# The 64-row remainder of wo, shared between tiles three and four of each query block

## The chip, the core and the metric

One core of a Trainium2 chip runs the whole kernel in one launch. The metric is device time in microseconds (us): the median of several executions. The profiler records one further execution, and its times are given from the start of that execution's span.

## What is computed

A transformer layer whose two branches run side by side on the same normalised input. There are 2048 tokens, a width of 448, 16 heads of 28, an attention window of 256, and a feed-forward width of 1792.

```python
def _A_ref(x, wqkv, wo):
    ...
    scores = jnp.einsum("bhqd,bhkd->bhqk", q, k) * (Dh ** -0.5)
    mask = (idx[:, None] - idx[None, :] >= 0) & (idx[:, None] - idx[None, :] < W)
    scores = jnp.where(mask[None, None], scores, -1e9)
    p = _softmax(scores, axis=-1)
    o = jnp.einsum("bhqk,bhkd->bhqd", p, v)
    return (lambda x, *d: x.transpose(*d))(o, 0, 2, 1, 3).reshape(B, S, D) @ wo
def _B_ref(x, w_gate, w_up, w_down):
    return (_gelu(x @ w_gate) * (x @ w_up)) @ w_down
x = A_x
xn = _layernorm(x, axis=-1)
return x + _A_ref(xn, A_wqkv, A_wo) + _B_ref(xn, B_w_gate, B_w_up, B_w_down)
```

## The kernel before

The tokens are worked on in four query blocks of 512, `qb` 0 to 3, each of four tiles (`tt` 0 to 3) of 128 tokens. Every engine executes its instructions in the order in which the program issues them; no scheduler reorders them (`manual_schedule`).

For each block there is an attention stage of ten steps (four heads at a time, `steps_of`), then a gated stage (`gated`). In a step TensorE computes the scores `sc` into the only score buffer (L653), ScalarE takes the exponential (L657) into `p_sb`, and VectorE multiplies the edges by masks (`apply_masks`, L573). While ScalarE works, TensorE executes what the list `plan` holds for that step: `(g, n)` is n further pieces of a generator. One generator, `gen_pairs`, projects q, k and v of the next block; another, `gen_up`, is the up half of the feed-forward of the last block (tile `ue`); and `gen_down(qb - 1)` is the output of the block before. So the output of blocks 0, 1 and 2 is computed in the attention of blocks 1, 2 and 3, and the output of block 3 alone at the end of the kernel.

`gen_down` makes the output of a 128-token tile as one sum in PSUM, `po`, 448 wide: 14 terms of `wd` with the gated hidden layer `hT`, and 4 terms of `wo` with the attention's output `oN`. 448 rows are three and a half times 128, so the fourth `wo` term has only 64 rows. `o_finish` (L357) prepares it on GpSimd. For blocks 0 to 2 it copies those 64 rows of tile 1 into the upper 64 partitions, and clears these for tiles 2 and 3. Tiles 0 and 1 then do their 64-row terms as a pair (L408): one in the upper, one in the lower half of the array's rows. Tiles 2 and 3 each do a 128-row term of which half is zero. In block 3 the upper half is cleared for all tiles and all four terms have 128 rows. Tile 3 of block 3 is computed in two halves of 224 columns, `first` and `last`, in tiles called `pl`, so that only a narrow add and store are left at the end. `end` adds the input `x_sb` to the sum on VectorE (L381, tile `res`) and issues the store on SyncE (L384).

PSUM has four banks for `po`, `pq`, `pk`, `pv`, `ov`, `ue` and `u`. `take` takes the bank that was given back first, `give` puts one back at the end of the list; both happen as the program is written out, and on the chip a matmul that starts a sum in a bank waits until the bank's last reader is done.

Of the kernel before, what the change touches and what calls it, by code (L numbers as in the profile page):

```python
# [17 lines left out]
P = 128  # L18
# [9 lines left out]
def kernel(  # L28
# [328 lines left out]
    def o_finish(qb):  # L357

        oN = oNs[qb]
        if qb < NB - 1:  # L360
            nc.gpsimd.memset(oN[64:128, 3, 2 * P:QB], 0.0)
            nc.gpsimd.tensor_copy(out=oN[64:128, 3, P:2 * P], in_=oN[0:64, 3, P:2 * P])
        else:
            nc.gpsimd.memset(oN[64:128, 3, :], 0.0)

    def gen_down(qb):

        hT, oN = hTs[qb], oNs[qb]
        fs = [(hT, wd, f) for f in range(NF)]
        main, late, os = fs[0:5] + fs[7:12], [fs[f] for f in (5, 12, 6, 13)], [(oN, wo, g) for g in range(4)]  # L370

        def begin(tt, lo=0, up=D):
            return tt, take("po", up - lo), lo, up

        def end(tt, po, lo, up):
            t, w = 4 * qb + tt, up - lo
            if lo:
                res = work.tile([P, 2 * QB], bf16, name="res", tag="wa", bufs=1)
            else:
                res = work.tile([P, D], bf16, name="res", bufs=4)  # L380
            nc.vector.tensor_tensor(out=res[:, 0:w], in0=po[:, 0:w], in1=x_sb[:, t, lo:up], op=ALU.add)  # L381
            if id(po) in held:
                give(po)
            nc.sync.dma_start(out=outv[:, t, lo:up], in_=res[:, 0:w])  # L384
            last_res[:] = [res]

        def part(o, terms, start=False, stop=False):
            tt, po, lo, up = o
            w = up - lo
            for n, (x, wt, k) in enumerate(terms):  # L390
                nc.tensor.matmul(po[:, 0:w], lhsT=x[:, k, tt * P:(tt + 1) * P], rhs=wt[:, k, lo:up],  # L391
                                 start=start and n == 0, stop=stop and n == len(terms) - 1, skip_group_check=True)
                if stop and n == len(terms) - 1:
                    end(*o)
                yield

        def whole(terms, *o):
            yield from part(begin(*o), terms, True, True)

        if qb < NB - 1:  # L400
            two = [begin(tt) for tt in range(2)]
            for o in two:
                yield from part(o, main + late, True)
            for o in two:
                yield from part(o, os[0:3])
            for tt, po, *_ in two:
                r = slice(64 * tt, 64 * tt + 64)
                nc.tensor.matmul(po, lhsT=oN[r, 3, tt * P:(tt + 1) * P], rhs=wo[r, 3, :], start=False, stop=True,  # L408
                                 tile_position=(64 * tt, 0), skip_group_check=True)
            for o in two:  # L410
                end(*o)
            yield
            for tt in (2, 3):
                yield from whole(main + late + os, tt)
        else:
            two = [begin(tt) for tt in range(2)]
            for terms, start in ((main, True), (late, False)):
                for o in two:
                    yield from part(o, terms, start)
            first, last = ((3, phase[0].pool.tile([P, 2, QB], f32, name="pl", tag="s")[:, 0, 0:D // 2], lo, lo + D // 2)  # L420
                           for lo in (0, D // 2))
            yield from part(first, main + late, True)
            for o in (*two, first):
                yield from part(o, os, False, True)
            yield from part(last, main, True)
            yield from whole(main + late + os, 2)
            yield from part(last, late + os, False, True)

    def new_hT(qb):
# [156 lines left out]
    def attention(qb, plan):  # L586
# [54 lines left out]
        for i, (scores, ncol, edges) in enumerate(steps):  # L641
            assert (qb, scores[-1][0]) in done
            if i in pvs:
                pv(pvs[i])
            while fresh:
                apply_masks(*fresh.pop(0))
            ss = phase[0].pool.tile([P, 4, QB], f32, name="sc", tag="s")
            p_sb = work.tile([P, 4, QB], bf16, name="p_sb", bufs=5)
            for g, half, kt, q0, nq, col in scores:
                k0, nk = (64 * half, 64) if half is not None else (0, P)  # L650
                for j in range(4):
                    r = slice(32 * j, 32 * j + Dh)
                    nc.tensor.matmul(ss[k0:k0 + nk, j, col:col + nq], lhsT=kT[r, g, kt * P + k0:kt * P + k0 + nk],  # L653
                                     rhs=qT[r, g, ring(qb).start + q0:ring(qb).start + q0 + nq], start=True, stop=True,
                                     tile_position=(32 * j, k0), skip_group_check=True)
                parts.setdefault(g, []).append((half, kt, q0, nq, col, p_sb))
            nc.scalar.activation(out=p_sb[:, :, 0:ncol], in_=ss[:, :, 0:ncol], func=ACT.Exp, scale=SCALE)  # L657
            flush()
            if qb:
                fresh.append((p_sb, edges))  # L660
            else:
                for m in edges:
                    masked(p_sb, *m)
            while later:
                scale_o(*later.pop(0))
            for n in plan[i]:
                if n == "sums":
                    sums()
                elif n == "inverse":
                    inverse()  # L670
                elif n == "masks":
                    apply_masks(*fresh.pop(0))
                elif n == "scale":
                    scale_o(*later.pop(0))
                if not isinstance(n, tuple):
                    if callable(n):
                        n()
                    continue
                for _ in range(n[1]):
                    next(n[0], None)  # L680
# [120 lines left out]
    for qb in range(NB):  # L801
# [4 lines left out]
        if qb == 0:  # L806
            new_hT(0)
            early = (0, 1, 2, 3, 4)
            u = chain(gen_qk((1, 2, 3), {1: (3, pvs[3]), 2: (2, pvs[2])}), gen_up(0, (1, 2, 3, 0, 4), (3, 4)))
            w = gen_pairs(1, (("v", 0), ("v", 2), ("k", 0), ("k", 1), ("k", 2)))  # L810
            plan = [[(u, 2), ahead, (u, 1)], [lambda: v_dense(2, pvs[2]), (u, 2), ahead2, (u, 1)],
                    [lambda: spare.append(spare.pop(1)), (u, 2), ahead3, (u, 4)], [lambda: stat(8), (u, 11)],
                    [lambda: stat(9), (u, 7), lambda: stat(10), (u, 7), lambda: fill_pads(True)], ["sums", (u, 7)],
                    ["inverse", "scale", (w, 11)], [(w, 10)],
                    [lambda: stat(11), (w, 7), lambda: rstd(8, 4), "sums", "inverse", (w, 7)]]
        else:
            d = gen_down(qb - 1)
            if qb < 3:
                u = gen_pairs(qb + 1, (("v", 0), ("k", 0), ("v", 2), ("k", 1), ("k", 2)))
                plan = [[(d, 14)], [(d, 11)], [(d, 11)], [(u, 7)], [(d, 18)], ["sums", (u, 7), "inverse"], [(u, 11)],  # L820
                        [lambda: q_last(qb + 1, nc.vector.tensor_copy), (d, 6), "sums"], [(d, 2), "inverse", (d, 10)],
                        [(u, 9), "masks", (u, 1)]]
                plan[3] = [(d, 1), (u, 7)]
                if qb == 2:
                    plan[0], plan[2] = [(d, 13)], [(d, 10)]
                if qb == 1:
                    for i, j in enumerate((0, 1, 2, 4)):
                        plan[j].insert(0, lambda t=12 + i: stat(t))
                    plan[4].append(lambda: rstd(12, 4))
                    plan[1] = plan[1][:1] + [lambda: q_last(1, nc.vector.tensor_copy), (d, 8)]  # L830
                    plan[2] = plan[2][:1] + [(d, 12), lambda: collect(1)]
                    plan[4].append(lambda: deliver(1))
            else:
                new_hT(3)
                early = (1, 2, 3, 4, 5, 6)
                u = gen_up(3, early, (4, 6))
                plan = [[(u, 12)], [(u, 9)], [(d, 12)], [(d, 10)], [(d, 12)], [(d, 1), (u, 7), "sums"], [(d, 12), "inverse"],
                        ["sums", "inverse", (d, 12)], [(d, 12)], [(u, 13), "masks", (u, 1)]]
        if qb in (1, 2):
            swap(qb + 1)  # L840
        score_pool(1)
# [186 lines left out]
```

## Time and profile before

| | us |
|---|---|
| median of 3 runs | 213.64 (213.34 to 214.03) |
| the profiled execution's own time | 213.22 |
| its span, first to last instruction | 211.5 |
| TensorE busy in it | 206.6 |
| VectorE busy | 156.8 |
| ScalarE busy | 131.6 |
| GpSimd busy | 48.9 |

A row of the timeline gives the start, the time from the first instruction's start to the last one's end, the engine, the line, the operation and how many instructions are merged; in brackets stands how long the engine sat idle before it and what released it. On TensorE consecutive matmuls overlap in these records, so what one costs is the distance between starts, not its duration. A row of the chain of waits gives start, length, engine, tile, line and count.

### The profile page before, as it was taken

To read this page: it belongs to the slowest core of one execution; us is meant where nothing else is said; L and a number is where in the kernel's file an instruction comes from. 1 tells how busy PE (TensorE), PEld (TensorE's weight loads), DVE (VectorE), ACT (ScalarE), POOL (GpSimd) and SP (SyncE) were. 2 spreads that over 40 slices of the span, in tenths; PEclk is the share of its full clock that TensorE was granted. 3 is DMA by queue.
4 is the path that set the end of the run, shared out by engine and by line. 5 is a ranking of instruction groups with operands and counts; after the bars stand their busy time and mean duration, and the time that the engine had idled before them with its cause. 6 is when DMAs were issued, how large, how long until landed. Compare 5 with 4: busy or idle time off the path is not lost.

```text
span 211.5 us, 6340 instructions
## 1 busy us (share of the span) xinstructions
PE 206.6 (98%) x2682; PEld 97.4 (46%) x2682; DVE 156.8 (74%) x355; ACT 131.6 (62%) x123; POOL 48.9 (23%) x86
## 2 busy tenths in 40 slices
PE   7999999999999999999999999999999999999994
PEld 2333444444454545444445444544444454544562
DVE  6899988999767985696437897395384699659722
ACT  4699488566677977413778787523577786757000
POOL 5388658451100220041000112013000022005100
PEclk9999999999999999999999999999999999999999
DMA  6999989969410101003521000100100011000011
GB/s 167 289 236 203 108 212 221 220 189 223 111 47 29 39 11 34 9 4 67 74 75 47 25 0 27 22 0 16 31 3 0 10 41 41 7 3 0 22 60 39
DMA packets 24889, 15.67 MB, mean 74 GB/s; under 512 B 9208, under 2 KB 24728, under 8 KB 24856
## 3 DMA queue, kind: packets, MB, share of 16 engines
q1 hardware_dynamic: 23814, 14.87, 32.3%
q8 instruction: 22, 0.36, 0.7%
q10 hardware_dynamic: 1042, 0.34, 0.7%
q14 instruction: 11, 0.09, 0.2%
HBM read 9.26 MB, written 2.41 MB: 55 GB/s over the span
## 4 chain that ended last, share of the span: by engine, by line
PE 94%; DVE 2%; ACT 1%; DMA 1%; issue 0%; DVEq 0%; ACTq 0%
PE po L391 24%; PE gt L457 20%; PE u L457 12%; PE ue L457 8%; PE pq L333 7%; PE sc L653 7%; PE ov L625 5%; PE pv L319 4%; PE pq L190 2%; PE pl L391 2%; DVE st L155 1%; DMA x_sb<-in_A_x_dram 1%; PE pv L190 1%; ACT p_sb L657 1%; PE s L190 1%; PE pk L190 1%
## 5 line engine op out<-in xcount | busy, mean ns | idle before, releaser
L657 ACT ACTIVATE p_sb<-sc 128x2048 bf16<-128x2048 f32 x39 | 73.2, 1878 | 20.6 <-PE sc L653 14.4
L497 ACT ACTIVATE p_sb<-gt 128x1024 bf16<-128x1024 f32 x28 | 28.7, 1024 | 33.7 <-PE gt L457 30.7
L592 POOL TENSOR_TENSOR oN<-oc,l 128x512 bf16<-128x512 f32 x16 | 21.6, 1354 | 119.0 <-DVE l L605 119.0
L457 PE MATMUL gt<-xnT,wg 64*128 64x512 bf16 x224 | 45.6, 376 | 0.0
L391 PE MATMUL po<-wd,hT 128*128 128x448 bf16 x210 | 43.3, 353 | 0.0
L457 PE MATMUL gt<-xsw,wg 64*128 64x512 bf16 x168 | 40.7, 376 | 0.0
L505 DVE TENSOR_TENSOR hT<-p_sb,u 128x512 bf16<-128x512 bf16 x34 | 21.9, 677 | 16.0 <-PE u L457 15.8
L573 DVE TENSOR_TENSOR p_sb<-p_sb,masks 128x256 bf16<-128x256 bf16 (+1 forms) x90 | 27.8, 364 | 7.6 <-ACT p_sb L657 7.6
L391 PEld LDWEIGHTS <-hT 128*128 128x128 bf16 x238 | 21.9, 98 | 19.4 <-issue 2.2
L457 PEld LDWEIGHTS <-wg 64*128 64x128 bf16 x392 | 19.0, 94 | 22.5 <-issue 0.2
L457 PEld LDWEIGHTS <-wu 64*128 64x128 bf16 x392 | 18.8, 94 | 22.4 <-issue 1.0
L457 PE MATMUL u<-xnT,wu 64*128 64x512 bf16 x136 | 28.1, 376 | 0.0
L457 PE MATMUL u<-xsw,wu 64*128 64x512 bf16 x102 | 24.7, 376 | 0.0
L457 PE MATMUL ue<-xnT,wu 64*128 64x512 bf16 x88 | 18.0, 377 | 0.0
L381 DVE TENSOR_TENSOR res<-po,x_sb 128x448 bf16<-128x448 f32 x15 | 9.0, 619 | 11.5 <-PE po L391 11.0
L653 PE MATMUL sc<-qT,kT 28*64 28x320 bf16 (+7 forms) x648 | 16.4, 261 | 0.1
L457 PE MATMUL ue<-xsw,wu 64*128 64x512 bf16 x66 | 16.3, 377 | 0.0
L583 POOL TENSOR_SCALAR_AFFINE_SELECT p_sb<-p_sb 128x512 bf16<-128x512 bf16 (+1 forms) x21 | 14.2, 705 | 5.9 <-ACT p_sb L657 5.8
L610 DVE TENSOR_TENSOR oc<-oc,ov 128x512 f32<-128x512 f32 x12 | 8.2, 681 | 8.6 <-ACT oc L609 8.6
L653 PEld LDWEIGHTS <-kT 28*64 28x64 bf16 (+1 forms) x648 | 7.5, 102 | 13.3 <-issue 12.0
L474 DVE CAST hT<-ue 128x512 bf16<-128x512 f32 x18 | 11.6, 679 | 1.8 <-PE ue L457 1.8
L391 PE MATMUL po<-wo,oN 128*128 128x448 bf16 x54 | 12.0, 352 | 0.0
(110 smaller groups left out, 278.9 us busy)
## 6 DMA issues: line engine op xcount, KB each, us to landing
out_dram<-res SPq DMA_DIRECT2D x15, 112.0 KB
wd<-in_B_w_down_dram SPq DMA_DIRECT2D x2, 784.0 KB
x_sb<-in_A_x_dram SPq DMA_DIRECT2D x3, 448.0 KB
xsw<-xnT SPq DMA_DIRECT2D x6, 192.0 KB
wu<-in_B_w_up_dram SPq DMA_DIRECT2D x4, 224.0 KB
wg<-in_B_w_gate_dram SPq DMA_DIRECT2D x2, 448.0 KB
wu<-in_B_w_up_dram SPq DMA_DIRECT2D x2, 336.0 KB
wg<-in_B_w_gate_dram SPq DMA_DIRECT2D x2, 336.0 KB
```

What stands on the lines that cost most here:

```text
L190: nc.tensor.matmul(ps, lhsT=lhs(c), rhs=rhs(c), start=start and c == 0, stop=stop and c == 2, skip_group_check=True)
L333: nc.tensor.matmul(ps, lhsT=w.rearrange("p h d -> p (h d)"), rhs=xchunk(qb, hi, c, qb * QB, QB), start=c == 0, stop=c == 6, tile_position= ...
L391: nc.tensor.matmul(po[:, 0:w], lhsT=x[:, k, tt * P:(tt + 1) * P], rhs=wt[:, k, lo:up], start=start and n == 0, stop=stop and n == len(term ...
L457: nc.tensor.matmul(ps, lhsT=w[64 * hi:64 * hi + 64, c, p * P:(p + 1) * P], rhs=xchunk(qb, hi, c, qb * QB, QB), start=c == 0, stop=c == 6, ...
L474: copy(out=hTs[qb][:, p + 7 * i, :], in_=us[i])
L497: nc.scalar.activation(out=ges[p][:, :, :], in_=gt[:, :, :], func=ACT.Gelu_apprx_tanh)
L505: nc.vector.tensor_tensor(out=hT[:, p + 7 * i, :], in0=ge[:, i, :], in1=u, op=ALU.mult)
L573: nc.vector.tensor_tensor(out=reg, in0=reg, in1=m, op=ALU.mult)
L583: nc.gpsimd.affine_select(out=reg, in_=reg, pattern=mid + [[1 if diag else -1, min(w, P)]], compare_op=ALU.is_ge, fill=0.0, base=0 if diag ...
L592: nc.gpsimd.tensor_tensor(out=oN[:, g, :], in0=oc[:, :], in1=inv, op=ALU.mult)
L653: nc.tensor.matmul(ss[k0:k0 + nk, j, col:col + nq], lhsT=kT[r, g, kt * P + k0:kt * P + k0 + nk], rhs=qT[r, g, ring(qb).start + q0:ring(qb) ...
L657: nc.scalar.activation(out=p_sb[:, :, 0:ncol], in_=ss[:, :, 0:ncol], func=ACT.Exp, scale=SCALE)
```

## The change

- `o_finish`: one GpSimd copy of the 64 rows of tiles 1 and 3 into the upper half, for every block; both clearings go.
- `gen_down` for blocks 0 to 2: three 128-row `wo` terms for each tile (`os` has 3 in place of 4), and tiles 2 and 3 do the fourth as a pair (`half`). In block 2 both sums wait in PSUM until the pair. In blocks 0 and 1 tile 3's 64-row term is computed early, in a bank that is given back at once: VectorE adds `x_sb` to it and writes `xo`, in float32, over columns of `hT` that are no longer read; the closing add takes `xo` in place of `x_sb`.
- `gen_down` for block 3: the five 64-row matmuls (tile 2's, the two halves of tile 3's, and those of tiles 0 and 1) stand in one run before `last` and tile 2, whose sums they begin.
- `plan`: the counts follow. In blocks 1 and 2 step 4 has 17 pieces, step 5 has `"sums"` ahead of the pair, and step 8 one piece less. In the attention of block 3 steps 7 and 8 have one piece less, and the pair stands at the head of step 9, where the masks of step 8, before in front of the step's scores, come behind the two adds. In block 1 one `stat` moves from step 4 to step 2.
- `gen_up`: pair 5's second copy out of `ue` moves from VectorE to ScalarE.

```diff
-        if qb < NB - 1:
-            nc.gpsimd.memset(oN[64:128, 3, 2 * P:QB], 0.0)
-            nc.gpsimd.tensor_copy(out=oN[64:128, 3, P:2 * P], in_=oN[0:64, 3, P:2 * P])
-        else:
-            nc.gpsimd.memset(oN[64:128, 3, :], 0.0)
+        up, low = (oN[r, 3, :].rearrange("p (a b n) -> p a b n", b=2, n=P)[:, :, 1, :] for r in (slice(0, 64), slice(64, 128)))
+        nc.gpsimd.tensor_copy(out=low, in_=up)
...
-        main, late, os = fs[0:5] + fs[7:12], [fs[f] for f in (5, 12, 6, 13)], [(oN, wo, g) for g in range(4)]
+        main, late, os = fs[0:5] + fs[7:12], [fs[f] for f in (5, 12, 6, 13)], [(oN, wo, g) for g in range(3)]
...
-        def end(tt, po, lo, up):
+        def four(a):
+            return a.rearrange("p (a b) -> p a b", a=4)
+
+        def end(tt, po, lo, up, rest=None):
...
-            nc.vector.tensor_tensor(out=res[:, 0:w], in0=po[:, 0:w], in1=x_sb[:, t, lo:up], op=ALU.add)
+            if rest is None:
+                nc.vector.tensor_tensor(out=res[:, 0:w], in0=po[:, 0:w], in1=x_sb[:, t, lo:up], op=ALU.add)
+            else:
+                nc.vector.tensor_tensor(out=four(res[:, :]), in0=four(po), in1=rest, op=ALU.add)
...
+        def half(hi, o, start, stop):
+            tt, po, lo, up = o
+            r = slice(64 * hi, 64 * hi + 64)
+            nc.tensor.matmul(po[:, 0:up - lo], lhsT=oN[r, 3, tt * P:(tt + 1) * P], rhs=wo[r, 3, lo:up], start=start, stop=stop,
+                             tile_position=(64 * hi, 0), skip_group_check=True)
...
-            for tt in (2, 3):
-                yield from whole(main + late + os, tt)
+            third = begin(2)
+            yield from part(third, main + late + os, True)
+            if qb == NB - 2:
+                fourth = begin(3)
+                yield from part(fourth, main + late + os, True)
+            else:
+                fourth = begin(3)
+            half(0, third, False, True)
+            half(1, fourth, qb < NB - 2, True)
+            end(*third)
+            if qb == NB - 2:
+                end(*fourth)
+                yield
+                return
+            xo = hT[:, 0:4, 0:D // 2].bitcast(f32)
+            nc.vector.tensor_tensor(out=xo, in0=four(fourth[1]), in1=four(x_sb[:, 4 * qb + 3, :]), op=ALU.add)
+            give(fourth[1])
+            yield
+            fourth = begin(3)
+            for n, _ in enumerate(part(fourth, main + late + os, True)):
+                if n < 16:
+                    yield
+            end(*fourth, xo)
+            yield
...
+            third = begin(2)
             for o in (*two, first):
-                yield from part(o, os, False, True)
-            yield from part(last, main, True)
-            yield from whole(main + late + os, 2)
+                yield from part(o, os)
+            for hi, o in enumerate((*two, third, first, last)):
+                half(hi % 2 if hi < 4 else 1, o, o in (third, last), o not in (third, last))
+            for o in (*two, first):
+                end(*o)
+            yield from part(last, main)
+            yield from part(third, main + late + os, False, True)
             yield from part(last, late + os, False, True)
...
-            while fresh:
+            while fresh and plan[i].count("masks") < 2:
                 apply_masks(*fresh.pop(0))
...
-                plan = [[(d, 14)], [(d, 11)], [(d, 11)], [(u, 7)], [(d, 18)], ["sums", (u, 7), "inverse"], [(u, 11)],
-                        [lambda: q_last(qb + 1, nc.vector.tensor_copy), (d, 6), "sums"], [(d, 2), "inverse", (d, 10)],
+                plan = [[(d, 14)], [(d, 11)], [(d, 11)], [(u, 7)], [(d, 17)], ["sums", (d, 1), (u, 7), "inverse"], [(u, 11)],
+                        [lambda: q_last(qb + 1, nc.vector.tensor_copy), (d, 6), "sums"], [(d, 2), "inverse", (d, 9)],
...
-                u = gen_up(3, early, (4, 6))
+                u = gen_up(3, early, (4, 5, 6))
...
-                        ["sums", "inverse", (d, 12)], [(d, 12)], [(u, 13), "masks", (u, 1)]]
+                        ["sums", "inverse", (d, 11)], [(d, 11)], [(d, 1), "masks", (u, 13), "masks", (u, 1)]]
```

More of the change, by code (lines that the diff above doesn't have):

```diff
@@ L395, in part @@
                 yield
-        def whole(terms, *o):
-            yield from part(begin(*o), terms, True, True)
+        def half(hi, o, start, stop):
[3 more added lines that the diff above has]
+                             tile_position=(64 * hi, 0), skip_group_check=True)
         if qb < NB - 1:
@@ L405, in gen_down @@
                 yield from part(o, os[0:3])
[L406 to L409, printed above, removed]
+            for hi, o in enumerate(two):
+                half(hi, o, False, True)
             for o in two:
@@ L826 @@
                 if qb == 1:
-                    for i, j in enumerate((0, 1, 2, 4)):
+                    for i, j in enumerate((0, 1, 2, 2)):
                         plan[j].insert(0, lambda t=12 + i: stat(t))
@@ L830 @@
                     plan[1] = plan[1][:1] + [lambda: q_last(1, nc.vector.tensor_copy), (d, 8)]
-                    plan[2] = plan[2][:1] + [(d, 12), lambda: collect(1)]
+                    plan[2] = plan[2][:2] + [(d, 12), lambda: collect(1)]
                     plan[4].append(lambda: deliver(1))
```

## The prediction

> **What bounds the kernel now.** I read the page first, then TensorE's waits, then the chain of waits for what a matmul costs, then the timeline at each place that the change touches.
>
> ```profile
> span 211.5 us, 6340 instructions
> PE 206.6 (98%) x2682; PEld 97.4 (46%) x2682; DVE 156.8 (74%) x355; ACT 131.6 (62%) x123; POOL 48.9 (23%) x86
> PE 94%; DVE 2%; ACT 1%; DMA 1%; issue 0%; DVEq 0%; ACTq 0%
> ```
>
> The matmul engine is busy 98% of the span and makes 94% of the chain that ends last. Its whole list of waits has two rows, both from the start of the kernel:
>
> ```profile
> PE wps L150 <- DVE wo L124: 1.4, 1, 1.4
> PE pv L190 <- ACT xnT L186: 0.4, 1, 0.4
> ```
>
> So after the opening TensorE never waits for anyone. The time is the sum of its matmuls, and a matmul taken out is worth its whole distance to the next one, as long as no new wait appears. The chain gives that distance:
>
> ```profile
> 194.85 5.40 PE po L391 x28
> 200.26 1.34 PE pl L391 x14
> ```
>
> A 448-wide matmul takes 5.40/28 = 0.193 us, a 224-wide one 1.34/14 = 0.096 us.
>
> **The change, part by part. The pairs in blocks 0, 1 and 2.** Each block loses two 128-row matmuls, 2 x 0.193 = 0.386 us, and gains one pair of 64-row matmuls in different halves of the array. The kernel has that pair already, for tiles 0 and 1, in the very surroundings that the new ones get: behind scores, ahead of other 64-row work.
>
> ```profile
> 60.53 0.42 PE L653 MATMUL sc<-qT,kT 28*64 28x320 bf16 x16
> 60.89 0.36 PE L408 MATMUL po<-wo,oN 64*128 64x448 bf16 x2
> 61.09 0.35 PE L319 MATMUL pv<-wv,xnT 64*128 64x448 bf16 x1
> ```
>
> Both start in one row, and the next work starts 0.20 us later: the two halves do run side by side. A block saves 0.386 - 0.20 = 0.186 us, three blocks 0.56 us.
>
> **The run at the end.** In block 3 the fourth `wo` term now costs three 448-wide and two 224-wide matmuls, 3 x 0.193 + 2 x 0.096 = 0.77 us. Afterwards there are two rounds: tiles 0 and 1 together, then tile 2 in one half of the rows while `first` and `last` (224 each) follow one another in the other, 2 x 0.20 = 0.40 us. But here 128-row work stands on both sides, so TensorE changes from 128-row to smaller tiles and back. The nearest rows:
>
> ```profile
> 165.59 1.30 PE L391 MATMUL po<-wo,oN 128*128 128x448 bf16 x6
> 166.82 0.42 PE L653 MATMUL sc<-qT,kT 28*64 28x320 bf16 x16
> ...
> 194.26 0.59 PE L457 MATMUL gt<-xnT,wg 64*128 64x512 bf16 x3
> 194.79 1.50 PE L391 MATMUL po<-wd,hT 128*128 128x448 bf16 x7
> ```
>
> Six 448-wide matmuls take 1.16 us, and the scores start 1.23 us after the first: 0.07 us for the change to smaller tiles. On the way back, 194.26 opens on the second half of one 64-row pair and holds one more pair; pairs follow each other at 1.51/7 = 0.216 us (a `gt` of 14 takes 1.51 in the chain below), so 0.43 is work and 0.10 of the 0.53 us is the change. I take 0.17 us for both: 0.77 - 0.40 - 0.17 = 0.20 us saved. Bounds: 0.37 if the changes are free, 0.10 if `last` finds no overlap. Tile 2's last add becomes tighter, being followed by 7 narrow matmuls in place of 8:
>
> ```profile
> 207.90 0.62 DVE L381 TENSOR_TENSOR res<-po,x_sb 128x448 bf16<-128x448 f32 x1 [3.82 <-PE po L391]
> ...
> 208.66 0.39 DVE L381 TENSOR_TENSOR res<-pl,x_sb 128x224 bf16<-128x224 f32 x1
> ```
>
> The add takes 0.62 us and 7 x 0.096 = 0.67 us cover it. The last store follows as before.
>
> The Trainium skill, TensorEngine Tiling (Array Packing), Key Properties, says that changing the tiling mode drains TensorE. By the row, a 448-wide matmul lasts about 0.35 us and the next starts at 0.193, so a full drain would be 0.16 us a change, where the trace shows 0.07 and 0.10; by the full drain the end would save 0.05 us and the whole change 0.61 us.
>
> **GpSimd's copy.** In blocks 0 to 2 it takes the place of a clearing and a copy. In block 3 it is new in one respect: the clearing needed only that the rows had been sent off, the copy needs them delivered.
>
> ```profile
> 95.66 1.38 SPq L355 DMA_DIRECT2D oN<-o  x4
> 98.31 0.28 POOL L362 COPY oN<-oN 64x128 bf16<-64x128 bf16 x1 [1.42 <-DMA oN<-o]
> ...
> 197.43 1.36 SPq L355 DMA_DIRECT2D oN<-o  x4
> ...
> 201.44 1.68 PE L391 MATMUL po<-wo,oN 128*128 128x448 bf16 x8
> ```
>
> In block 1 the copy starts 98.31 - 95.66 = 2.65 us after the first of these issues; in block 3 that is 200.1. Twice the width is at most 0.56 us, done by 200.7, and the 64-row run starts some 1.5 us after the 201.44 of the other terms (six of 0.193 and three of 0.096). Hidden; 2 us would have to go wrong.
>
> **Blocks 0 and 1: the extra add and the banks.** VectorE has one 448-wide add more per block. The nearest rows are the same add with a bf16 result, 0.62 us, and the 512-wide float32 add `oc`, 0.69 us; I take 0.62. What matters is who waits. Written out, the bank list has tile 2 in one bank and the early term in another; the q and k pair that follows takes the other two, and then `ov` (attention's second `pv`) takes exactly these two. So that `pv` now stands behind both adds.
>
> ```profile
> 63.77 1.88 ACT L657 ACTIVATE p_sb<-sc 128x2048 bf16<-128x2048 f32 x1
> ...
> 61.28 1.16 DVE L381 TENSOR_TENSOR res<-po,x_sb 128x448 bf16<-128x448 f32 x2 [0.25 <-PE po L408]
> ...
> 67.70 0.82 DVE L573 TENSOR_TENSOR p_sb<-p_sb,masks 128x256 bf16<-128x256 bf16 x3
> 68.44 0.70 DVE L598 STREAM_TRANSPOSE l<-oc 128x512 f32<-128x512 f32 x1
> 69.18 0.26 DVE L599 RECIPROCAL inv_all<-l 128x16 f32<-128x16 f32 x1
> 70.58 0.69 DVE L610 TENSOR_TENSOR oc<-oc,ov 128x512 f32<-128x512 f32 x1
> ...
> 67.05 0.42 PE L653 MATMUL sc<-qT,kT 28*64 28x320 bf16 x16
> 67.41 0.39 PE L333 MATMUL pq<-xnT,wqp 64*128 64x512 bf16 x1
> 69.03 0.74 PE L625 MATMUL ov<-p_sb,v_sb 64*32 64x256 bf16 x48
> ```
>
> In the order of after, VectorE does the masks of step 4, the transpose and the reciprocal ahead of the adds. The exponential ends at 65.65; 0.82 + 0.70 + 0.26 later it is 67.4. Step 4 has one matmul less, so the scores start at 66.86, the pair at 67.22, and the adds can start 0.39 us behind the pair (60.89 to 61.28): 67.61. VectorE is free 0.2 us earlier. Two adds take 1.16 us: 68.77. `pv` comes 0.20 (pair) + 1.62 (67.41 to 69.03) after the pair's place: 69.04. That leaves 0.27 us, and I cost it at nothing. If VectorE reached the adds 0.5 us late, the difference would be a stall of TensorE. The `stat` moved to step 2 only empties VectorE before this point.
>
> **Scores against the exponential.** There is one score buffer, so scores wait for the exponential before them. Four steps (8 in blocks 1 and 2, 7 and 8 in block 3) lose 0.193 us of matmuls.
>
> ```profile
> 72.85 1.88 ACT L657 ACTIVATE p_sb<-sc 128x2048 bf16<-128x2048 f32 x1 [0.17 <-PE sc L653]
> 75.31 1.88 ACT L657 ACTIVATE p_sb<-sc 128x2048 bf16<-128x2048 f32 x1 [0.59 <-PE sc L653]
> ...
> 74.82 0.42 PE L653 MATMUL sc<-qT,kT 28*64 28x320 bf16 x16
> 77.55 0.43 PE L653 MATMUL sc<-qT,kT 28*64 28x320 bf16 x24
> ```
>
> Step 8's exponential ends at 77.19 and the next scores start at 77.55: 0.36 us are left, 0.17 afterwards. That 0.09 is enough is in the same rows: 72.85 + 1.88 = 74.73, and scores at 74.82 without a wait. In block 3, scores follow scores after 0.36 + 11 x 0.193 + 0.07 = 2.55 us, and the exponential starts about 0.5 us behind its scores and lasts 1.88: some 0.15 us are left. I cost it at nothing.
>
> **Step 9 of block 3.** Here the pair is followed by two adds, the late masks and two `ue` pairs.
>
> ```profile
> 178.26 3.15 PE ue L457 x28
> 181.41 1.51 PE gt L457 x14
> 182.92 1.26 PE ov L625 x81
> ...
> 181.47 0.58 ACT L474 CAST hT<-ue 128x512 bf16<-128x512 f32 x1 [1.15 <-PE ue L457]
> ```
>
> Call the start of the step's scores S. The pair is at S + 0.36, the adds run from S + 0.75 to S + 1.91. The second `ue` pair takes the adds' banks and starts at S + 0.36 + 0.20 + 1.51 = S + 2.07: 0.16 us to spare. Then VectorE has masks (0.82), one copy out of `ue` (bounded by the 448- and 512-wide rows above, 0.62 to 0.69), masks (0.82): all done by S + 4.3, and `pv` starts at S + 5.1. The copy moved to ScalarE is 0.58 us in the 1.15 us that ScalarE sat idle. Nothing is late; without that move VectorE would carry 0.7 us more here.
>
> **Sum.** 0.56 + 0.20 = 0.76 us off the profiled execution: 213.22 - 0.76 = 212.46. The median of the runs stands 0.42 us above that execution, so I forecast 213.64 - 0.76 = 212.88, which is 0.36% less.
>
> **The rivals.**
>
> 1. Part is lost: the 0.15 to 0.17 us of slack is not enough, at the four score steps or at step 9's bank, or `last` does not overlap. Four waits of 0.05 us and 0.10 at the end make 0.30: 213.64 - 0.46 = 213.18. For it: small margins. Against: 0.09 us already suffices, above.
> 2. Changes of tile shape cost a full matmul's tail, 0.16 us each, at the end: 213.64 - 0.61 = 213.03. For it: only the end puts 64-row work between 128-row work. Against: 0.07 and 0.10 in the rows. It is the Trainium skill's rule of draining, above.
> 3. Slower: VectorE becomes the bound at the second `pv` of blocks 1 and 2. The same masks that take 0.82 us also show this:
>
> ```profile
> 71.18 1.51 DVE L573 TENSOR_TENSOR p_sb<-p_sb,masks 128x256 bf16<-128x256 bf16 x3
> 70.73 1.27 POOL L592 TENSOR_TENSOR oN<-oc,l 128x512 bf16<-128x512 f32 x1 [14.27 <-DVE l L605]
> 172.50 1.87 DVE L573 TENSOR_TENSOR p_sb<-p_sb,masks 128x256 bf16<-128x256 bf16 x3
> ```
>
>    Masks beside a GpSimd product take up to 1.87, 1.05 us more. If the masks ahead of the adds did, the adds would end at 67.4 + 1.05 + 1.16 = 69.6 against `pv` at 69.04: 0.6 us in each of two blocks, 1.2 - 0.76 = 0.4 us slower, 214.1. It decides from 0.38 us of stall in a block on. Against: GpSimd has no product for 14.27 us before 70.73.
> 4. It does not do what it says: 64-row matmuls do not overlap and every pair costs 0.386. Then the blocks save nothing, and the end about nothing: 213.64. The 0.20 us behind L408 speaks against it.
>
> **How the numbers follow.** Forecast 0.60, rival 1 0.15, rival 2 0.12, rival 3 0.10, rival 4 0.03. About 0.3%, 0.64 us, is what a measurement of this kernel can tell from no change. The forecast lies only 0.12 us beyond it, so I leave 0.56 of its 0.60 on the faster side, with a third of rivals 1 and 2: 0.65 faster; 0.25 within; 0.10 slower. The forecast's own range is 212.7 (tile changes free, 0.93 saved) to 213.2. The whole range, with a little for the spread of the medians, is 212.4 to 213.8.
>
> **What would show it.** Right: L408's successor with 6 + 6 + 5 matmuls, 0.20 us to the next work; 128-row `wo` matmuls down from 54 to 45 and wide `pl` ones from 8 to 6; TensorE's waits still only those of the opening; the span about 0.76 us shorter, of which 0.2 behind the last `gt`. Wrong: a wait of `ov` or `ue` for the adds in VectorE, of scores for the exponential, or gaps above 0.1 us around the 64-row run at the end. The forecast fails if these come to 0.4 us or more.

## The result and the profile after

| | before | after |
|---|---|---|
| median of 7 runs, us | 213.35 (213.21 to 214.03) | 212.61 (212.50 to 212.84) |
| ratio | | 0.9964 (95%: 0.9953 to 0.9974) |
| profiled execution's own time, us | 213.22 | 212.69 |
| its span, us | 211.5 | 210.8 |

The changed kernel is 0.36% faster, 0.74 us between the medians. The page of after:

```profile
span 210.8 us, 6335 instructions
PE 205.1 (97%) x2678; PEld 96.5 (46%) x2682; DVE 157.8 (75%) x356; ACT 132.0 (63%) x124; POOL 48.4 (23%) x83
PE 94%; DVE 2%; ACT 1%; DMA 1%; issue 1%; DVEq 0%; ACTq 0%
```

TensorE still makes 94% of the chain. Its busy time is 1.5 us less, but four matmul records are missing in it (2678 matmuls beside 2682 weight loads), so that is not a measure of the gain. VectorE has 1.0 us more. The groups by line show what the output's `wo` terms have become:

```profile
L394 PE MATMUL po<-wo,oN 128*128 128x448 bf16 x45 | 10.3, 352 | 0.0
L403 PE MATMUL po<-wo,oN 64*128 64x448 bf16 x15 | 2.7, 359 | 0.0
L394 PE MATMUL pl<-wo,oN 128*128 128x224 bf16 x6 | 0.9, 259 | 0.0
L403 PE MATMUL pl<-wo,oN 64*128 64x224 bf16 x2 | 0.4, 256 | 0.0
L432 DVE TENSOR_TENSOR hT<-po,x_sb 128x448 f32<-128x448 f32 x2 | 1.2, 615 | 0.0
L384 DVE TENSOR_TENSOR res<-po,hT 128x448 bf16<-128x448 f32 x2 | 1.2, 625 | 1.6 <-PE po L394 1.6
L361 POOL COPY oN<-oN 64x256 bf16<-64x256 bf16 x4 | 1.6, 397 | 21.3 <-DMA oN<-o 15.9 <-DMA kT<-k 5.4
```

45 and 6 full matmuls in place of 54 and 8, and 17 half ones in place of 6. The early add (L432) takes 0.615 us and the closing one that reads it (L384) 0.625. TensorE's waits, the whole list:

```profile
PE wps L150 <- DVE wo L124: 1.4, 1, 1.4
PE tp L185 <- DVE xn L170: 0.5, 1, 0.5
PE pv L190 <- ACT xnT L186: 0.4, 1, 0.4
PE pq L190 <- issue: 0.2, 1, 0.2
```

The first three stand in the opening, in code that the change leaves as it was. The last is a q projection, also untouched, that waited for nothing that the profile shows; it stands in all five traces in which four matmul records are missing (after and e1 to e4) and in none of the other seven, so it is most likely the place of such a record. None is a wait for another engine in what the change touches.

The opening differs from one execution to the next, so traces are compared from a mark behind most of it: the first `ue` matmul. The second mark is the last block's run of 70 `gt`, the third the end of the chain. In the chain of waits of before, then of after:

```profile
18.53 0.65 PE ue L457 x6
...
187.30 7.55 PE gt L457 x70
...
209.06 0.56 issue
```

```profile
18.59 0.65 PE ue L488 x6
...
186.76 7.55 PE gt L488 x70
...
208.35 0.56 issue
```

From `ue` to `gt`, where the pairs of blocks 0 to 2 lie, 168.77 has become 168.17: 0.60 us less. From `gt` to the end, where the 64-row run lies, 21.76 has become 21.59: 0.17 us less. The sum is 0.77 us.

Of the 0.60 us, 0.03 are not the change's. From the first `ue` matmul to the scores behind the `ue` matmuls, in code that the change leaves as it was, before's profiled execution took 4.19 us (18.36 to 22.55 in its timeline), and each of the eleven other traces of this document 4.16. Without that the blocks gained 0.57 us, 0.19 in each of the three attention stages, and the whole change 0.74 us, as much as the medians say.

### The profile page after: what moved, and what is told of

The parts are those of the page before. It is cut to its first block, busy times and chain, and to the rows that moved or that the text cites. A ratio compares the mean times of both kernels' runs of the same rounds, so it can differ in the third digit from the quotient of the medians.

```text
span 210.8 us, 6335 instructions
## 1 busy us (share of the span) xinstructions
PE 205.1 (97%) x2678; PEld 96.5 (46%) x2682; DVE 157.8 (75%) x356; ACT 132.0 (63%) x124; POOL 48.4 (23%) x83
## 4 chain that ended last, share of the span: by engine, by line
PE 94%; DVE 2%; ACT 1%; DMA 1%; issue 1%; DVEq 0%; ACTq 0%
PE po L394 24%; PE gt L488 20%; PE u L488 12%; PE ue L488 8%; PE sc L684 7%; PE pq L333 7%; PE ov L656 5%; PE pv L319 4%; PE pq L190 2%; PE pl L394 2%; DVE st L155 1%; PE po L403 1%; DMA x_sb<-in_A_x_dram 1%; PE pv L190 1%; ACT p_sb L688 1%; PE s L190 1%
## 5 line engine op out<-in xcount | busy, mean ns | idle before, releaser
L382 DVE TENSOR_TENSOR res<-po,x_sb 128x448 bf16<-128x448 f32 x13 | 7.7, 621 | 7.7 <-PE po L403 4.4
L505 DVE CAST hT<-ue 128x512 bf16<-128x512 f32 x17 | 11.0, 678 | 1.3 <-PE ue L488 1.2
L170 DVE TENSOR_SCALAR xn<-x_sb,mv_all,rstd_all 128x448 bf16<-128x448 bf16 (+1 forms) x28 | 11.0, 434 | 0.3 <-ACT rstd_all L161 0.3
```

Of the source, the lines that this page charges most:

```text
L170: nc.vector.tensor_scalar(out=xf[:, lo:lo + n], in0=x_sb[:, t, src:src + n], scalar1=mv_all[:, t, 0:1], scalar2=rstd_all[:, t:t + 1], op0= ...
L505: copy(out=hTs[qb][:, p + 7 * i, :], in_=us[i])
```

## The experiments

All kernels were run beside the kernel before on the same chip. The marks below come from each one's chain of waits, worked out as above; each kernel has one trace. A difference of 0.03 us is the noise of such a stretch: two kernels with the same code between two marks never differed by more, and before and e2_blocks_old, the same up to the last `gt`, differ by just this much.

| kernel | ratio to before (95%) | `ue` to `gt` | `gt` to end |
|---|---|---|---|
| before | 1 | 168.77 | 21.76 |
| after | 0.9964 (0.9953 to 0.9974) | 168.17 | 21.59 |
| e1_end_old | 0.9969 (0.9957 to 0.9980) | 168.17 | 21.76 |
| e2_blocks_old | 0.9998 (0.9989 to 1.0007) | 168.74 | 21.59 |
| e3_pairs_together | 1.0021 (1.0012 to 1.0030) | 168.17 | 22.72 |
| e4_pairs_apart | 1.0050 (1.0032 to 1.0067) | 168.18 | 23.36 |
| e5_adds_late | 1.0021 (1.0011 to 1.0030) | 169.48 | 21.59 |
| e6_masks_front | 0.9974 (0.9965 to 0.9984) | 168.29 | 21.59 |
| e7_up_copy_vector | 0.9966 (0.9953 to 0.9979) | 168.17 | 21.59 |
| e8_neither | 0.9974 (0.9964 to 0.9983) | 168.31 | 21.58 |
| e9_two_later | 1.0056 (1.0039 to 1.0073) | 170.01 | 21.59 |
| e10_sums_behind | 0.9979 (0.9968 to 0.9990) | 168.52 | 21.59 |

### The two halves of the change alone

e1_end_old keeps the pairs of blocks 0 to 2 and gives block 3 its old end:

```diff
         oN = oNs[qb]
+        if qb == NB - 1:
+            nc.gpsimd.memset(oN[64:128, 3, :], 0.0)
+            return
...
-            third = begin(2)
-            for o in (*two, first):
-                yield from part(o, os)
...
+            for o in (*two, first):
+                yield from part(o, os + [(oN, wo, 3)], False, True)
+            yield from part(last, main, True)
+            yield from part(begin(2), main + late + os + [(oN, wo, 3)], True, True)
+            yield from part(last, late + os + [(oN, wo, 3)], False, True)
```

> The pairs of blocks 0, 1 and 2 as changed, block 3's end as before (four 128-row wo terms for each tile). My account by places: three pairs are worth 0.56 us, so about 0.26% faster than before, and the span is 0.16 to 0.20 us longer than the changed kernel's 210.8. If the end made the whole gain (pairs hidden by something else), this run equals before within 0.1 us; if the blocks made it all, it equals the changed kernel.

e2_blocks_old is the reverse: the kernel before with the new `o_finish` and the new end for block 3 alone.

> Only block 3's run of 64-row matmuls; blocks 0 to 2 and the plans as before. My account: 0.16 to 0.20 us faster than before (0.08%), all of it after the last gt. Changes of tile shape that drain fully leave 0.05 us; free ones give 0.37 us. Together with the run before it must make up the changed kernel's 0.7 us, if the two parts do not touch each other.

The marks fall out exactly: e1 has the changed kernel's 168.17 and before's 21.76, e2 before's 168.74 and the changed kernel's 21.59. The two parts are independent and add up: 0.57 us (after against e2's 168.74, which is without the 0.03 us of before's trace) and 0.17 us. The span foreseen for e1 was not met (211.7 in place of about 211.0); the profiled execution was the slowest of e1's seven (213.40 against a median of 212.72), and its trace says why:

```profile
19.31 0.65 PE ue L486 x6
...
187.48 7.55 PE gt L486 x70
```

Its opening alone took 19.31 us against 18.59. The medians see the first part (0.9969) and cannot see the second: 0.17 us is 0.08%, inside e2's interval, where full drains (0.05 us, a ratio of 0.9998) would also lie and no cost (0.37 us, 0.9983) would lie just outside. For the end only the marks decide.

### What a change of tile shape costs

Four more pairs are put into tile 2's sum at the end, with results in PSUM columns that nothing reads. `spare_pair` is two calls of `half` into the unused halves of the two `pl` tiles. In e3 all stand behind the first matmul:

```diff
-            yield from part(third, main + late + os, False, True)
+            for n, _ in enumerate(part(third, main + late + os, False, True)):
+                if n == 0:
+                    for _ in range(4):
+                        spare_pair()
+                yield
```

> The changed kernel with four more 64-row pairs in one place of tile 2's 128-row sum at the end (their results go into unused PSUM columns and are not used). One way in and one way out: 4 x 0.20 + 0.17 = 0.97 us longer than the changed kernel by my account; 0.8 + 0.32 = 1.12 with full drains; 0.8 if changes of tile shape are free.

e4 has `if n in (0, 4, 8, 12): spare_pair()` instead.

> The same four extra pairs in four places, four matmuls apart. By my account four ways in and out: 4 x (0.20 + 0.17) = 1.48 us longer than the changed kernel, 0.51 more than with the pairs together. With full drains 4 x 0.52 = 2.08 us; with free changes 0.8, the same as together.

Measured: 1.13 us with the pairs together, 1.77 apart. The three ways in and out that e4 has more cost 1.77 - 1.13 = 0.64 us, 0.21 each: above my 0.17, well below 0.32. The rows show where it goes (start of the first, length, count), first e3, then e4:

```profile
203.88 0.35 PE L394 MATMUL po<-wd,hT 128*128 128x448 bf16 x1
204.33 0.93 PE L403 MATMUL pl<-wo,oN 64*128 64x448 bf16 x8
205.19 1.12 PE L394 MATMUL po<-wd,hT 128*128 128x448 bf16 x5
```

```profile
204.57 0.93 PE L394 MATMUL po<-wd,hT 128*128 128x448 bf16 x4
205.44 0.36 PE L403 MATMUL pl<-wo,oN 64*128 64x448 bf16 x2
205.73 0.93 PE L394 MATMUL po<-wd,hT 128*128 128x448 bf16 x4
```

Four pairs and the way out take 0.86 us in e3, one pair and the way out 0.29 in e4: 0.19 us for a pair among pairs and 0.10 for the way out. Four 128-row matmuls and the way in take 0.87 us in e4. A 448-wide matmul takes 0.189 us, not 0.193: in before, 28 of them begin at 194.79 (a row of the prediction), and 5.30 us later, 5.30/28 = 0.189 for each, follows

```profile
200.09 1.50 PE L391 MATMUL pl<-wd,hT 128*128 128x224 bf16 x14
```

The chain's 5.40 us for the same 28 begins at 194.85, where the profile lets the `gt` before them end (194.26 + 0.59), and runs to the last one's end, so it is not the distance between starts. With 0.189 the way in is 0.87 - 0.76 = 0.11 us, and both ways are 0.21, as above.

At each change of shape the weights come late. Within the four 128-row matmuls of e4 the weights run ahead: all four loads are done at 205.06, the matmuls at 205.50. The loads of the pair at 205.44 start only with the pair itself:

```profile
204.57 0.49 PEld L394 LDWEIGHTS <-hT 128*128 128x128 bf16 x4 [0.20 <-issue]
205.43 0.10 PEld L403 LDWEIGHTS <-oN 64*128 64x128 bf16 x2 [0.37 <-issue]
```

Such a load takes 0.10 us, as much as a change costs. That it is the cause is not shown; no run separates it from a short drain.

The first pair of both kernels waits 0.16 us longer (0.45 behind the matmul ahead of it, 203.88 to 204.33 in e3, in place of 0.29). That is the experiment's own doing: it writes into the tile of `first`, which VectorE is still adding up in e3's trace:

```profile
203.89 0.38 DVE L382 TENSOR_TENSOR res<-pl,x_sb 128x224 bf16<-128x224 f32 x1
```

The add ends at 204.27 and the pair starts at 204.33. Without those 0.16 us e3 is at the 0.97 foreseen and e4 at 1.61, against 1.48.

The Trainium skill, TensorEngine Tiling (Array Packing), Key Properties, has TensorE drain at a change of mode. The trace agrees that there is a cost, and limits it: some 0.2 us for both ways together, not two whole matmul tails of 0.16 us (whose ends the profile only models).

### How close VectorE's adds are to TensorE's banks

e5_adds_late puts two more VectorE instructions ahead of the adds in blocks 0 and 1:

```diff
+            if qb < NB - 2:
+                for _ in range(2):
+                    pad = work.tile([P, nc.vector.BN_STATS_DIM], f32, name="pad", bufs=1)
+                    nc.vector.bn_stats(out=pad[:, :], in_=x_sb[:, 0, :])
             end(*third)
```

> The changed kernel with two more VectorE instructions (statistics of a tile, about 0.63 us each, result unused) ahead of the two adds in blocks 0 and 1. My account: VectorE reaches the adds at 68.7 in place of 67.65, the second ends at about 69.9, and ov, which takes the adds' banks, can start only then in place of 69.06: a stall of TensorE of about 0.8 us in each block, 1.6 to 1.7 us in all. Rival: VectorE is off the path here, 0 us, or at most the slack is larger than 0.26 and the stall correspondingly smaller.

It cost 1.31 us, 0.65 a block. The timeline of its VectorE and of its TensorE:

```profile
67.75 1.23 DVE L429 BATCH_NORM_STATS2 pad<-x_sb 128x6 f32<-128x448 bf16 x2
68.89 0.60 DVE L382 TENSOR_TENSOR res<-po,x_sb 128x448 bf16<-128x448 f32 x1
69.42 0.61 DVE L436 TENSOR_TENSOR hT<-po,x_sb 128x448 f32<-128x448 f32 x1
...
69.55 0.29 PE L660 MATMUL ov<-p_sb,v_sb 64*32 64x256 bf16 x4
70.08 0.73 PE L660 MATMUL ov<-p_sb,v_sb 64*32 64x256 bf16 x44 [0.24 <-DVE hT L436]
```

The early add ends at 70.03, and the rest of `ov` starts at 70.08: the mechanism is the one foreseen. The size is 0.15 us a block below it, mostly because the two extra instructions follow each other closely (the first add comes 1.14 us behind their start, not 1.26). The `ue` mark stands 0.37 us later in e5 than in after (18.96 and 18.59); less that, the early add ends 0.86 us later than after's 68.80. Of these 0.26 are slack, which leaves 0.60 to lose. Note that the trace books 0.24 us as a wait where 0.65 was lost: idle time counts only from the modelled end of the matmul before.

e10_sums_behind turns round one order that the change chose, `[(d, 1), "sums", (u, 7), "inverse"]` in place of `["sums", (d, 1), (u, 7), "inverse"]`:

> The changed kernel with the transpose and reciprocal of step 5 in blocks 1 and 2 behind the pair again, so behind the two adds on VectorE. The adds keep their time (second one done at 68.8), but the copy of k out of its bank comes after the transpose, ends at about 70.3 in place of 69.9, and the v projection that takes that bank stands at 70.1: TensorE loses 0.2 to 0.4 us in each block, 0.4 to 0.8 us in all. Rival: the place of these two instructions does not matter, 0 us.

It lost 0.35 us, just under the range given. In its trace k's copy out of its bank comes late, and the v projection behind it starts with one half of the array alone:

```profile
69.57 0.63 DVE L244 CAST kT<-pk 128x512 bf16<-128x512 f32 x1
...
70.03 0.36 PE L319 MATMUL pv<-wv,xnT 64*128 64x448 bf16 x1
70.25 0.37 PE L319 MATMUL pv<-wvs,xsw 64*128 64x448 bf16 x2
```

The copy ends at 70.20; the second half starts at 70.25, where the changed kernel has both at once. So the place of the transpose and the reciprocal is worth more than half of the 0.57 us that the pairs of blocks 0 to 2 bring.

### Step 9 of the last block

e6_masks_front puts the masks back in front of the scores (`while fresh:`, and `[(d, 1), (u, 13), "masks", (u, 1)]`).

> The changed kernel with the masks of step 8 in block 3's attention back in front of step 9's scores, so ahead of the adds. VectorE is free at 177.46 in the changed kernel; masks to 178.2, two adds to 179.3, while the second ue pair, which takes the adds' banks, starts at 179.35: no stall or up to 0.1 us. If the order of masks and adds carries the gain, it is 0.3 us or more slower than the changed kernel.

e7_up_copy_vector has `gen_up(3, early, (4, 6))`.

> The changed kernel with ue pair 5's second copy on VectorE again. VectorE has 0.6 us more between 179.7 and 181.6 and is still free about 1 us before ov: within 0.05 us of the changed kernel. If VectorE bounds this place, up to 0.6 us slower.

e8_neither has both edits.

> The changed kernel with the masks of step 8 in front of the adds and ue pair 5's second copy on VectorE, both. Alone the first cost 0.12 us between the first ue and the last gt of block 3, the second nothing. If the two are independent: 0.12 us. If VectorE's queue carries one delay into the other (masks, adds and two copies in a row, up to the banks that ov takes at about 183): 0.3 us or more.

By the marks the masks in front cost 0.12 us, the copy nothing (168.17), both together 0.14: independent, and the copy on ScalarE is not needed for the time. In e6's trace the adds end later than the second `ue` pair wants its banks:

```profile
178.26 1.15 DVE L382 TENSOR_TENSOR res<-po,x_sb 128x448 bf16<-128x448 f32 x2
...
179.46 0.47 PE L488 MATMUL ue<-xsw,wu 64*128 64x512 bf16 x2
```

The second add ends at 179.41, and the half that needs its bank starts at 179.46. TensorE's list of waits in this stretch is empty: the other half's matmul had started at 179.33 and ran on, so no idle time is booked. The intervals of e6, e7 and after overlap; these 0.12 us rest on the marks alone.

### Scores against the exponential

e9_two_later changes step 8 and 9 of blocks 1 and 2 from `(d, 9)]` and `[(u, 9)` to `(d, 7)]` and `[(d, 2), (u, 9)`.

> The changed kernel with two of step 8's pieces of the output moved to step 9 in blocks 1 and 2; no work added or taken away. The slack of scores against the exponential is 0.17 us in the changed kernel; without 2 x 0.193 of cover TensorE has to wait 0.2 to 0.3 us in each block, 0.4 to 0.6 us in all. Rival: the exponential's end does not bind there, 0 us.

It cost 1.84 us, three times the upper end of what was foreseen. The rows of e9's TensorE, then one of its VectorE:

```profile
74.98 0.42 PE L684 MATMUL sc<-qT,kT 28*64 28x320 bf16 x16
...
77.40 0.43 PE L684 MATMUL sc<-qT,kT 28*64 28x320 bf16 x24 [0.19 <-ACT p_sb L688]
77.77 0.55 PE L394 MATMUL po<-wo,oN 128*128 128x448 bf16 x2
78.25 0.39 PE L333 MATMUL pq<-xnT,wqp 64*128 64x512 bf16 x1
...
78.91 0.38 PE L333 MATMUL pq<-xnT,wqp 64*128 64x512 bf16 x1
79.47 0.37 PE L333 MATMUL pk<-xsw,wsq 64*128 64x512 bf16 x1 [0.18 <-DVE res L384]
...
77.38 1.50 DVE L604 TENSOR_TENSOR p_sb<-p_sb,masks 128x256 bf16<-128x256 bf16 x3 [0.54 <-ACT p_sb L688]
```

Scores follow scores after 2.42 us, where after's 2.54 less two matmuls would be 2.16: the exponential does bind, and takes 0.26 us, as foreseen. The rest is what the move brought along, and the account given for this run had none of it. The two matmuls now stand ahead of 64-row work, a change of shape of 0.10 us (0.48 less 2 x 0.189). And the next q and k pair takes the bank of tile 3, which VectorE gives back late: its add (78.80 to 79.41) now stands behind three masks that take 1.50 us, where in after it comes ahead of them (77.50). That makes 0.56 us between 78.91 and 79.47 in place of 0.216, 0.34 lost. From there the two halves run out of step up to the next other work, which costs another 0.2 us. Together 0.9 us in each of two blocks.

## Why the prediction was right

- **A matmul removed is worth its whole distance.** Held: each part gained what its matmuls were worth, and no wait of TensorE for another engine appeared outside the opening. e1 and e2 show that the parts do not lean on each other.
- **The pairs: 0.56 us forecast, 0.57 measured.** The pair's own rows were right (0.20 to the next work). Two small errors cancel. The 0.193 us of a 128-row matmul is 0.004 too much, 0.008 us for two. And the sum left out the way from scores into 64-row work. In before the first projection pair stands there, and the next follows 0.23 us behind it (67.41 in the prediction's rows, then):

```profile
67.64 0.38 PE L333 MATMUL pq<-xsw,wsq 64*128 64x512 bf16 x1
```

  In after the `wo` pair stands there, and the first projection pair is only 0.22 us long:

```profile
67.25 0.36 PE L403 MATMUL po<-wo,oN 64*128 64x448 bf16 x2
67.45 0.38 PE L333 MATMUL pq<-xnT,wqp 64*128 64x512 bf16 x1
67.67 0.38 PE L333 MATMUL pq<-xsw,wsq 64*128 64x512 bf16 x1
```

  That is some 0.01 us in each block: 2 x 0.189 - 0.20 + 0.01 = 0.19, three times 0.57.
- **The end: 0.20 us forecast, 0.17 measured.** The two changes of shape took 0.21 in place of 0.17 us (e3 and e4). The way in was read as 0.07 because six matmuls were counted at 0.193; with 0.189 the same rows give 0.10. `last` did overlap: in after the second round and the way out take 0.28 us.

```profile
202.41 0.55 PE L403 MATMUL po<-wo,oN 64*128 64x448 bf16 x3
202.62 0.35 PE L403 MATMUL pl<-wo,oN 64*128 64x224 bf16 x2
202.90 1.13 PE L394 MATMUL pl<-wd,hT 128*128 128x224 bf16 x10
```

- **The early add.** Foreseen from 67.61 to 68.77, with `ov` at 69.04. In after:

```profile
67.65 0.62 DVE L382 TENSOR_TENSOR res<-po,x_sb 128x448 bf16<-128x448 f32 x1 [0.19 <-PE po L403]
68.19 0.61 DVE L432 TENSOR_TENSOR hT<-po,x_sb 128x448 f32<-128x448 f32 x1
69.06 0.74 PE L656 MATMUL ov<-p_sb,v_sb 64*32 64x256 bf16 x48
```

  0.26 us to spare, and e5 shows that this slack is the right quantity: past it every delay of VectorE is TensorE's. Rival 3 named the place that would have turned the sign; its condition, slow masks just there, did not occur (0.83 us at 65.72). The `stat` moved to step 2 was not tried alone.
- **Scores against the exponential.** 0.17 us was left, and e9 shows that the limit is near where it was drawn: two more matmuls out, 0.38 us, and 0.26 us of waiting, so 0.12 of the 0.17 could be used.
- **Step 9.** The 0.16 us of slack was real (0.15 in after, 179.04 to 179.19): e6 delays the adds and loses 0.12. The copy on ScalarE, which the prediction counted as relief for VectorE, hides nothing (e7).
- **GpSimd's copy.** 0.40 us against a bound of 0.56, long before its reader; no matmul waited for it.
- **The other rivals.** The slack was not used up (rival 1): `ue` to `gt` gained the whole 0.57. The full drain (rival 2) was to cost 0.32 us for both ways; they took 0.21. That pairs do not overlap (rival 4) falls with e1, whose blocks gain as much, and with the 0.20 us from the pair at 67.25 to the next work at 67.45.

The sum of 0.76 us met 0.74 by the marks, without the 0.03 us that are not the change's, and 0.74 by the medians. The two times forecast were less near. The profiled execution took 212.69 us, 0.23 above 212.46: its span is 0.65 us shorter than before's (211.50 and 210.85), and the time outside the span 0.12 us longer. Before's median over seven runs is 0.29 us below that over the first three (213.35 and 213.64), which covers the 0.27 us between the 212.61 measured and the 212.88 forecast.

## What to carry to other kernels

Where one engine is busy without waits, count its instructions by the distance between starts, take the price of a new form from a place with the same neighbours, and spend the rest of the care on who takes which buffer next: here the gain of the blocks hung on adds that end 0.15 to 0.26 us before a matmul takes their bank. Work that costs nothing where it stands can cost half of the gain when it stands behind two adds (e10: 0.35 us). And compare traces from a mark behind the opening, where effects of 0.1 us that no median resolves are plain, and look between the marks for what the change did not touch.

## What the runs showed of the hardware

- Going from 128-row to 64-row matmuls and back cost 0.21 us (e4 against e3: 0.64 us for three times), a little more than one pair saves (0.19 us).
- A matmul whose bank comes late lets the other half of the array finish what it has begun; only a delay shorter than one matmul leaves that half on time (e6: its next matmul came at 179.55, 0.22 us behind the one at 179.33, the usual distance). A longer delay holds both (e9: both start again at 79.47). The pair then runs out of step to the next different work and loses 0.1 to 0.2 us, and the list of waits may show nothing (e6) or less than half of it (e5: 0.24 of 0.65 us).
- The opening of one and the same code took between 18.5 and 19.3 us to the first `ue` matmul in these traces. That is as much as the whole change, and its cause is open.
